# Layer 1's second product as seven block products over three groups of tokens

## The chip, the cores and the metric

The kernel runs on one core of one Trainium2 chip. The metric is device time in microseconds (us) of one execution. Engines are called by their names: TensorE (PE in the rows, its weight load PEld), VectorE (DVE), ScalarE (ACT), GpSimd (POOL), SyncE (SP, whose queue is SPq).

## The reference

Attention with a decay and a causal mask over 4 batches, 8 heads, 576 positions and 64 columns a head; then two layers, each with 2304 tokens, a width of 512 and an inner width of 2048, all in float32:

```python
x = attn(q, k, v, f)                      # 2304 x 512
g = np.maximum(0.01 * (x @ w_in), x @ w_in)
x = g @ w_out                             # layer 1's second product
h = x @ w_in2
x = (h / (1 + np.exp(-h))) @ w_out2       # layer 2
```

The weights come in as 64-bit numbers and are turned into float32 on the chip. A float32 product is made of three matmuls on fp32r parts: each operand is split into a high part (a cast on ScalarE) and a low part (a subtraction, `less`, on VectorE or GpSimd), and high x high, high x low and low x high are summed in PSUM.

## The kernel before

The program holds its own planner, `Plan` (L82). Generators yield operations with an engine, a cost and a rank; the planner runs them in its own time and writes each engine's instructions in the order in which they come out. So the order on every engine, SyncE's transfers included, is fixed ahead. The lowest rank goes first where several operations are ready; `either` (L131) chooses between GpSimd and VectorE by the earlier planned end, with a bonus of 0.3 us for GpSimd. The costs are formulas: `dve_cost` (L244) is 0.07 + 1.042e-3 n us, `pool_cost` 0.1 + 2.2e-3 n. `take` and `give` count buffers; `wait` and `signal` order generators.

The stages overlap. Attention ends near 365 us; layer 1's first product (`hidden`, L929, the hidden product) fills TensorE beside it and runs alone until 404. It goes over eight chunks of tokens; each gated result goes to DRAM as `g1_d`. `conv_out` (L1581), from attention's middle on, turns W_out into float32 in two lines and stores it in `wo_d`; `out_weights` (L1031) loads and splits its 16 row blocks into the weight slots as the last chunk of the hidden product frees them.

The second product, `summed` (L1091), goes over five groups of tokens (256 and 4 x 512). `first_values` (L1054) loads g1 (`gl`) into four buffers and splits it (`gs`) into three. Per group TensorE runs 16 row blocks x 4 column blocks x 3 terms into four PSUM banks; `finish` (L1121) copies the sums out and stores them as `x1_d`.

Layer 2 already uses seven block products. Its first one, `hidden2` (L1338), has 3 groups of 2 x 384 tokens, 8 column pairs and 6 matmuls of 384 columns for each of the seven; its second one, `summed2` (L1477), has matmuls of 256 columns. `fetch2` (L1648) loads its weights' words, `combos` converts and mixes them with four VectorE operations of 256 columns (`sub`, L1174) per pair of row blocks, `second_weights` stores the seven combinations in `w2_d` and `fills` loads and splits them into 28 homes (`unit`, L1619), first for W_in and, as its tiles are used up, for W_out.

Of the kernel before, what the change touches and what calls it, by code (L numbers as in the profile page):

```python
# [53 lines left out]
SUMS = ((0, 256), (256, 512), (768, 512), (1280, 512), (1792, 512))  # L54
SET_A = ("sp", "sp", "sp", "av")
# [205 lines left out]
def fused_kernel(ctx, tc, qt, kt, va, vb, ft, w1, wi2, wo2, out):  # L261
# [9 lines left out]
    NCS = len(SUMS)  # L271
# [21 lines left out]
    wo_d = dram.tile([FF, 128, DM], F32, name="wo_d")  # L293
# [3 lines left out]
    w2_d = dram.tile([2, 128, 2 * NU, 256], F32, name="w2_d")  # L297

    ident = const.tile([128, 128], F32, name="ident")
    zmask = const.tile([128, ZOFF + 256], F32, name="zmask")  # L300
# [241 lines left out]
    at = {}  # L542
# [345 lines left out]
    def attention():  # L888
# [18 lines left out]
        w2t["a"] = ctx.enter_context(tc.tile_pool(name="w2a", bufs=1, side="right"))  # L907
# [100 lines left out]
    def gate(j, s):  # L1008
# [15 lines left out]
        yield dma(1024 * n, lambda: nc.sync.dma_start(out=g1_d[s, :, :, o:o + n], in_=g))  # L1024
# [6 lines left out]
    def out_weights():  # L1031
        def split(f, w, i):
            i_y = yield take("wy", WY_BUFS)
            y = decp["wo"].tile([128, DM], F32, tag="wy", name="wz", bufs=WY_BUFS)
            yield dma(262e3, lambda: nc.sync.dma_start(out=y, in_=wo_d[f]), 0)
            yield copy(DM, w[:, 0], y, "a", 0)
            yield less(DM, w[:, 1], y, f32(w[:, 0]), "pd", 0, PE_LAT)
            give("wy", i_y)
            wo_h[f] = w, i
            signal(("woh", f))  # L1040

        yield wait("weights")
        for f in range(FF):
            i = yield take(("w", ROOM_W[f]), 1)
            w = slot(ROOM_W[f], [128, 2, DM], F32R, "wo")
            p.start(split(f, w, i))
        yield wait(*[("woh", f) for f in range(FF)])
        wo_es.close()
        w2t["b"] = ctx.enter_context(tc.tile_pool(name="w2b", bufs=1))
        signal("decoded")  # L1050

    gs = {}

    def first_values():  # L1054

        yield wait(("ring_free", max(j for j in range(NCH) if j % 2 == 0)))

        def split(j, s, n, cuts, src, i):
            flat = src.rearrange("p a t -> p (a t)")
            for parts in cuts:  # L1060
# [11 lines left out]
        def splits():  # L1072
            yield wait("gated")
            for j, (_, n) in enumerate(SUMS):
                for s in range(NST):
                    yield wait(("gl", j, s))
                    yield from split(j, s, n, ((0, 1),) if n <= T else ((0,), (1,)), *loaded.pop((j, s)))
# [727 lines left out]
```

## Time and profile before

| | us |
|---|---|
| median of 3 runs | 969.61 (967.44 to 971.61) |
| the profiled execution | 969.07 |
| its span, first to last instruction | 967.3 |
| TensorE busy | 955.8 |
| VectorE busy | 669.3 |
| ScalarE busy | 573.7 |
| GpSimd busy | 56.1 |

Busy time counts an instruction from start to end; matmuls overlap in the engine, so the mean duration of one (390 ns for 512 columns) is longer than the time that it adds to a row of them. The pace of a loop is read from busy time by count. Idle time stands in front of the instruction that came late, with the one that released it.

### The profile page before, as it was taken

How to read it: one execution, taken by the hardware profiler on the slowest of the kernel's cores; microseconds unless marked ns; L12 is line 12 of the kernel's file. 1: busy time of each engine (PE TensorE's matmuls, PEld its weight loads, DVE VectorE, ACT ScalarE, POOL GpSimd, SP SyncE). 2: the span in 40 equal slices, each digit the busy share in tenths (PEclk: the TensorE clock that was granted, in tenths of full speed). 3: DMA queues.
4: the chain of work that ended last, by engine and by line, in shares of the span. 5: the costliest groups of instructions: out<-in, count | busy, mean ns of one | idle time of the engine just before them, and what ended most of it. 6: DMA issues, size and time to landing. Idle time of an engine off the chain costs nothing.

```text
span 967.3 us, 18030 instructions
## 1 busy us (share of the span) xinstructions
PE 955.8 (99%) x6433; PEld 878.2 (91%) x6433; DVE 669.3 (69%) x1645; ACT 573.7 (59%) x1296; POOL 56.1 (6%) x73
## 2 busy tenths in 40 slices
PE   9999999999999999999999999999999999999998
PEld 8787998889888989998888888999999999999998
DVE  5998786698669940477787677424144488998884
ACT  7978787788578842644343345546456665454441
POOL 2001220122013000000000000000000020000000
PEclk9999999999999999999999999999999999999999
DMA  7943543476666634789888887552366674554442
GB/s 216 288 130 89 168 155 103 136 229 208 207 188 229 217 117 152 252 305 328 328 306 300 293 319 256 190 192 98 122 205 218 218 221 128 153 154 140 126 128 67
DMA packets 140374, 190.50 MB, mean 197 GB/s; under 512 B 9446, under 2 KB 105342, under 8 KB 140252
## 3 DMA queue, kind: packets, MB, share of 16 engines
q1 hardware_dynamic: 139852, 188.95, 60.3%
q8 instruction: 51, 0.84, 0.4%
q10 hardware_dynamic: 432, 0.39, 0.1%
q14 instruction: 39, 0.32, 0.1%
HBM read 122.79 MB, written 66.50 MB: 196 GB/s over the span
## 4 chain that ended last, share of the span: by engine, by line
PE 77%; DVE 10%; DMA 6%; ACT 5%; issue 2%; SPq 0%; DVEq 0%; ACTq 0%
PE m L1338 18%; PE m L1477 17%; PE acc L1107 17%; PE hpw L929 12%; PE sps L711 4%; PE av L860 4%; PE tps L792 3%; DMA qk<-in_kt_dram 2%; DMA wst<-in_wo_dram 2%; DVE sc L691 2%; ACT sc L734 1%; DMA wst<-in_w_dram 1%; PE hps L929 1%; ACT sc L744 1%; DVE sc L742 1%
## 5 line engine op out<-in xcount | busy, mean ns | idle before, releaser
L929 PE MATMUL hpw<-ring,w 128*128 128x320 f32 (+1 forms) x1344 | 216.0, 303 | 0.1
L1107 PE MATMUL acc<-gs,wo 128*128 128x512 f32 (+1 forms) x960 | 199.0, 369 | 0.7 <-ACT gs L1065 0.4
L1107 PEld LDWEIGHTS acc<-gs,wo 128*128 128x128 f32 x960 | 167.3, 189 | 30.6 <-ACT gs L1065 0.6
L929 PEld LDWEIGHTS hpw<-ring,w 128*128 128x128 f32 x1344 | 189.1, 190 | 2.0 <-issue 1.0
L1338 PE MATMUL m<-xa,w 128*128 128x384 f32 x576 | 113.9, 339 | 1.0 <-ACT m L1364 0.8
L1477 PE MATMUL m<-w,xa 128*128 128x256 f32 x924 | 113.2, 281 | 0.7 <-DVE xa L340 0.6
L1477 PEld LDWEIGHTS m<-w,xa 128*128 128x128 f32 x924 | 110.7, 188 | 1.4 <-DVE xa L340 1.3
L734 ACT ACTIVATE sc<-sc,st 128x576 f32<-128x576 f32 (+4 forms) x160 | 93.1, 582 | 25.2 <-DVE st L691 24.3
L1338 PEld LDWEIGHTS m<-xa,w 128*128 128x128 f32 x576 | 102.0, 188 | 2.3 <-ACT m L1364 1.1
L691 DVE CUSTOM_DVE_ANT_0 sc<-sps,zmask 128x288 f32<-128x288 f32 (+4 forms) x160 | 71.1, 449 | 32.6 <-PE sps L711 23.9
L1065 ACT CAST gs<-gl 128x512 fp32r<-128x512 f32 x72 | 44.6, 621 | 72.2 <-PE acc L1107 66.5
L1338 PE MATMUL m<-xb,w 128*128 128x384 f32 x432 | 86.9, 336 | 0.0
L325 ACT CAST xa<-g 128x512 fp32r<-128x512 f32 x88 | 49.5, 568 | 47.8 <-PE m L1477 22.8
L1338 PEld LDWEIGHTS m<-xb,w 128*128 128x128 f32 x432 | 76.2, 188 | 0.3 <-ACT z L1378 0.2
L1477 PE MATMUL m<-w,xb 128*128 128x256 f32 x588 | 74.1, 283 | 0.3 <-DVE xb L340 0.3
L1477 PEld LDWEIGHTS m<-w,xb 128*128 128x128 f32 x588 | 72.0, 192 | 0.6 <-DVE xb L340 0.5
L792 PE MATMUL tps<-ident,sc 66*107 66x66 f32 (+3 forms) x480 | 67.7, 269 | 1.6 <-ACT sc L744 1.0
L711 PE MATMUL sps<-m,s 66*128 66x288 f32 (+9 forms) x288 | 66.8, 313 | 1.5 <-DVE st L691 0.8
L1174 DVE TENSOR_TENSOR g<-g 128x256 f32<-128x256 f32 x144 | 61.5, 430 | 8.9 <-DMA g<-g_d 8.0
L340 DVE TENSOR_TENSOR gs<-gl,gs 128x512 fp32r<-128x512 f32 x72 | 49.5, 688 | 23.4 <-ACT gs L1065 23.2
L1022 ACT ACTIVATE gw<-hpw 128x320 f32<-128x320 f32 (+1 forms) x112 | 45.1, 410 | 30.9 <-PE hpw L929 27.2
L792 PEld LDWEIGHTS tps<-ident,sc 66*107 66x107 f32 (+3 forms) x480 | 55.5, 152 | 7.8 <-ACT sc L744 1.8
(129 smaller groups left out, 1308.8 us busy)
## 6 DMA issues: line engine op xcount, KB each, us to landing
g_d<-z SPq DMA_DIRECT2D x24, 768.0 KB
g<-g_d SPq DMA_DIRECT2D x36, 512.0 KB
gl<-g_d SPq DMA_DIRECT2D x32, 512.0 KB
w_d<-f SPq DMA_DIRECT2D x16, 896.0 KB
ws<-w_d SPq DMA_DIRECT2D x56, 256.0 KB
g_d<-gw SPq DMA_DIRECT2D x32, 320.0 KB
wst<-in_w_dram SPq DMA_DIRECT2D x17, 512.0 KB
g_d<-gw SPq DMA_DIRECT2D x32, 256.0 KB
```

The costliest lines, as they stand in the source:

```text
L325: ("act", act_cost(n, base), lambda: nc.scalar.copy(dst, src), 0.0),
L340: ("dve", dve_cost(n), lambda: nc.vector.tensor_tensor(dst, a, b, op=ALU.subtract), 0.0),
L691: yield dve(w, lambda: nc.vector.tensor_tensor_reduce(out=sc[0:qn, k0:k0 + w], in0=ps[0:qn], in1=zmask[0:qn, z0:z0 + w], scale=-0.125, sca ...
L711: nc.tensor.matmul(ps[0:qn], ht[x][:, qs], ht[y][:, k0:k0 + w], start=r == 0, stop=r == len(ops) - 1)
L734: yield act(kn, lambda: nc.scalar.activation(sc[0:qn, 0:kn], sc[0:qn, 0:kn], ACTF.Exp, scale=-1.0, bias=st[0:qn, 2 * i + a:2 * i + a + 1], ...
L792: nc.tensor.transpose(ps[0:k1 - k0, o:o + qn], ht["p"][i][0:qn, k0:k1], ident[0:qn, 0:qn])
L929: nc.tensor.matmul(dst, w[:, wi, c * 128:(c + 1) * 128], x(xi, c), start=(first_ and c == 0 and r == 0), stop=(c == KC - 1 and r == 2), sk ...
L1022: yield act(n, lambda: nc.scalar.activation(g[:, part], hp_t, ACTF.Prelu, alpha=0.01), 1, 0.05)
L1107: nc.tensor.matmul(acc[c], w[:, wi, c * 128:(c + 1) * 128], g[:, gi], start=(f == 0 and r == 0), stop=(f == FF - 1 and r == 2), skip_group ...
L1174: ("dve", dve_cost(n), lambda: nc.vector.tensor_tensor(dst, a, b, op=op_), 0.0),
L1338: nc.tensor.matmul(dst, w[:, wi, c * 128:(c + 1) * 128], x[:, xi, c], start=start and c == 0 and r == 0, stop=stop and c == 1 and r == 2, ...
L1477: nc.tensor.matmul(banks[b][:, e], t[:, gi, a * 128:(a + 1) * 128], w[:, wi], start=begin and a == 0 and r == 0, stop=jp == NP // 2 - 1 an ...
```

## The change

Layer 1's second product g @ W_out is cut into 2 x 2 blocks in all three directions: the inner width into 2 x 1024, the output columns into 2 x 256, and the tokens into three groups of 2 x 384. Per group, seven block products stand for eight, on sums and differences of the blocks of g and of W_out.

- W_out: `conv_out` is one line with one buffer. For each of eight pairs of row blocks it converts both, mixes them (`mix`, four VectorE operations of 256 columns) and stores the seven combinations in a third part of `w2_d`. `fills(0)` loads and splits them into the 28 homes that layer 2's weights take later; W_in of layer 2 moves into a home when the last group has used it.
- g: `quarters` loads the blocks a11, a21, a22 and a12 of a group in 4 pieces each (128 x 2 x 384, 48 loads in all) into three sets of homes, which later groups and other blocks take over. `made` and `prep` build the sums in place: x5 = a21 + a22 (VectorE or GpSimd), x6 = x5 - a11, x3 = a12 - x6, x7 = a22 - x6, and split each operand into one of four buffers (`SPLITS`): 84 splits of 768 columns.
- `summed` runs the products in the order of `G_TURN`, 12 matmuls of 384 columns for each piece. `sums` copies partial sums between PSUM banks (seed) and out of them, and adds.
- Layer 2's W_out words are fetched only after product 2 of the last group. Layer 2's tiles move to other homes, its operand combinations are formed in place in another order, and the splits in `fills` may all go to GpSimd.

```diff
-SUMS = ((0, 256), (256, 512), (768, 512), (1280, 512), (1792, 512))
-SET_A = ("sp", "sp", "sp", "av")
+GQ = (1, 5, 6, 2, 7, 4, 3)
+G_TURN = (
+    ((1, 0), (5, 1), (6, 2), (2, 3), (7, 4), (4, 6), (3, 7)),
+    ((1, -2), (6, 1), (5, 2), (2, 3), (7, 4), (4, 6), (3, 7)),
+    ((1, -2), (6, 1), (5, 2), (2, 3), (7, 4), (4, 5), (3, 6)),
+)
+SPLITS = 4
+X_ON = "pd"
...
-    wo_d = dram.tile([FF, 128, DM], F32, name="wo_d")
...
-    w2_d = dram.tile([2, 128, 2 * NU, 256], F32, name="w2_d")
...
+    w2_d = dram.tile([3, 128, 2 * NU, 256], F32, name="w2_d")
...
-        yield dma(1024 * n, lambda: nc.sync.dma_start(out=g1_d[s, :, :, o:o + n], in_=g))
+        yield dma(1024 * n, lambda: nc.sync.dma_start(out=g1_d[s, :, :, o:o + n], in_=g), -1 if j > NCH - 3 else 1)
...
-    def out_weights():
...
-    def first_values():
...
+    def q_group(n, name):
+        return {"11": 0, "21": 1 + n % 2, "12": 1 + n % 2, "22": 2 - n % 2}[name]
+
+    def quarters():
+
+        yield wait("decoded")
+        todo = [(0, "11"), (0, "21"), (0, "22")]
+        for n in range(NG):
+            todo += [(n, "12")]
+            if n + 1 < NG:
+                todo += [(n + 1, "11"), (n + 1, "21"), (n + 1, "22")]
...
+                def load(n, name, s, sg, o, t):
+                    yield dma(393e3, lambda: nc.sync.dma_start(out=t, in_=g1_d[sg, :, :, o:o + TB]), 0)
+                    signal(("q", n, name, s))
+
+                p.start(load(n, name, s, sg, o, quarter(grp, s)))
+
+    g_order = sorted((7 * n + pos, n, q) for n in range(NG) for q, pos in G_TURN[n])
...
+    def q_used(n, name, s, uses):
+
+        k = n, name, s
+        left[k] = left.get(k, uses) - 1
+        if not left[k]:
+            grp = q_group(n, name)
+            give(("q", grp, s), q_count.setdefault((grp, s), 0))
+            q_count[grp, s] += 1
+            if n == NG - 1 and name != "21":
+                signal(("q_gone", grp, s))
+
...
+    def made(n, s):
+
+        a11, a21, a22 = (quarter(q_group(n, k), s) for k in ("11", "21", "22"))
+        yield wait(("q", n, "21", s), ("q", n, "22", s))
+        yield sub(2 * TB, a21, a21, a22, X_ON, 0, ALU.add)
+        signal(("x5", n, s))
+        yield wait(("gx", n, 1, s))
+        yield sub(2 * TB, a11, a21, a11, "d", 0)
+        signal(("x6", n, s))
+        q_used(n, "21", s, 2)
...
+    def prep(n, q, s, i):
+        a = {k: quarter(q_group(n, k), s) for k in ("11", "12", "21", "22")}
+        t = w2t["s", i % SPLITS]
+        src, name = None, None
...
+            src = a["11"]
+        elif q == 4:
+            yield wait(("q", n, "22", s))
+            src = a["22"]
+        elif q == 2:
+            yield wait(("q", n, "12", s))
+            src = a["12"]
+        else:
+            yield wait(("x3", n, s))
+            src = a["12"]
+        yield act(2 * TB, lambda: nc.scalar.copy(t[:, 0], src), 0, 0.09)
+        yield less(2 * TB, t[:, 1], src, f32(t[:, 0]), "d", 0, PE_LAT)
+        gx[n, q, s] = t, i
+        signal(("gx", n, q, s))
+        if q == 5:
+            q_used(n, "21", s, 2)
+        elif q == 7:
+            q_used(n, "22", s, 2)
+            q_used(n, "11", s, 1)
+        elif q == 4:
+            q_used(n, "22", s, 2)
+        elif q == 2:
+            yield wait(("x6", n, s))
+            yield sub(2 * TB, a["12"], a["12"], a["11"], "d", 0)
+            yield wait(("gx", n, 6, s))
+            signal(("x3", n, s))
+        elif q == 3:
+            q_used(n, "12", s, 1)
+
+    def preps():
+        yield wait("decoded")
+        for n in range(NG):
+            for s in range(SF):
+                p.start(made(n, s))
+        for _, n, q in g_order:
+            for s in range(SF):
+                i = yield take("split", SPLITS)
+                p.start(prep(n, q, s, i))
+
+    G_BANKS = (("sp", "sp"), ("sp", "av"), ("h", "h"), (("acc", 0), ("acc", 1)))
+
+    def g_bank(n, role, j):
+        return bank(G_BANKS[(3 * n + (0, 2, 1)[role]) % 4][j], [128, TB], "acc")
...
-            yield wait("hidden" if j else "attention")
...
-                    yield op("pe", mm_cost(n, 3), lambda: product(c), 1, 0)
...
+            if q == 5:
+                yield wait("hidden", ("second", n, 0), ("second", n, 1))
+                for j in range(2):
+                    held[n][j][1] = yield from g_bank(n, 1, j)
+                signal(("third", n))
+            need = {1: None, 2: "seed1", 6: "seed1", 7: "two1", 4: "three1", 5: None, 3: "four1"}[q]
+            role, start, stop = {
+                1: (0, True, False), 2: (0, False, True), 6: (2, False, False), 7: (2, False, False),
+                4: (2, False, True), 5: (1, True, False), 3: (1, False, True),
+            }[q]
+            for s in range(SF):
+                k = SF * GQ.index(q) + s
+                yield wait(("gx", n, q, s), ("wu", k))
+                x, i = gx[n, q, s]
+                w = wu[k]
...
+                    def product():
+                        for e in range(2):
+                            for r, (wi, xi) in enumerate(((0, 0), (0, 1), (1, 0))):
+                                nc.tensor.matmul(
+                                    dst, w[:, e, wi, j * 128:(j + 1) * 128], x[:, xi, e],
+                                    start=start and s == 0 and e == 0 and r == 0,
+                                    stop=stop and s == SF - 1 and e == 1 and r == 2, skip_group_check=True,
+                                )
+
+                    yield op("pe", 6 * MMB, product, 1 if "hidden" in p.seen else 2, 0)
+                    if s == SF - 1:
+                        signal(("m1", n, j, q))
+                give("split", i)
...
+    def sums(n, j, held):
+        c_t, c_h = held[0]
+        held[2] = yield from g_bank(n, 2, j)
+        signal(("second", n, j))
...
+        yield wait(("m1", n, j, 1))
+        yield act(TB, lambda: nc.scalar.copy(y_t, c_t), -1, 0.1)
+        signal(("seed1", n, j))
...
+        yield wait(("m1", n, j, 5))
+        v_t, v_h = held[1]
+        yield dve(TB, lambda: nc.vector.tensor_tensor(z, v_t, z, op=ALU.add), -1)
+        signal(("four1", n, j))
+
...
+
+        p.start(fourth())
+        yield wait(("m1", n, j, 4))
+        p.start(evict(y_t, 1, j, y_h))
+        yield wait(("m1", n, j, 3))
+        yield dve(TB, lambda: nc.vector.tensor_tensor(u, v_t, u, op=ALU.add), 0)
+        give(*v_h)
...
+    def mix(f, b12, rank):
+        yield sub(HW, f[:, 4], f[:, b12], f[:, 0], "d", rank)
+        yield sub(HW, f[:, b12], f[:, 3], f[:, b12], "d", rank)
+        yield sub(HW, f[:, 5], f[:, 3], f[:, 4], "d", rank)
+        yield sub(HW, f[:, 6], f[:, 3 - b12], f[:, 5], "d", rank)
+
...
+    def conv_out():
+        out_d = w2_d[0].rearrange("p (s f) n -> p s f n", s=7)
+        for j in range(FF // 2):
+            yield wait(("words1", j, 0))
+            i_f = yield take("wf", 1)
+            f = decp["wo"].tile([128, 7, HW], F32, tag="wf", name="wf", bufs=1)
+            y = f[:, 4:6].rearrange("p s n -> p (s n)")
+            for e in range(2):
+                yield wait(("words1", j, e))
+                src, i_s = words1.pop((j, e))
+                t = f[:, 2 * e:2 * e + 2].rearrange("p s n -> p (s n)")
+                yield from to_f32(t, src, y, t, 2, True)
+                give("wst", i_s)
+            yield from mix(f, 1, 2)
+            yield dma(918e3, lambda: nc.sync.dma_start(out=out_d[:, :, j], in_=f), 2)
+            give("wf", i_f)
+            signal(("spilt", 0, j))
...
-    UNIT_AT = ["ring1"] * 4 + [("w", r) for r in ROOM_W] + ["g"] * 3 + ["ring0"] * 4 + [("u", 0)]
+    UNIT_AT = ["ring0"] * 4 + [("w", r) for r in ROOM_W] + [("u", 0)] + ["ring1"] * 4 + ["g"] * 3
...
+            if which:
+                yield wait(("m1", NG - 1, 1, 2))
...
+    def fills(which):
+        for u in range(NU):
+            if which == 0:
+                q, s = GQ[u // SF], u % SF
+                at_ = 8 * W_SLOT[1][q] + 2 * s
+                yield wait(*[("spilt", 0, 2 * s + e) for e in range(2)])
+            else:
+                at_ = 2 * u
+                both = (2 * u, 2 * u + 1)
+                yield wait(*[("spilt", which, n // 7) for n in both])
+                yield wait(*([("used", n // 7, W_Q[0][n % 7]) for n in both] if which > 1 else [("used1", u)]))
+                units[which - 1, u][1]()
+            t = yield from unit(which, u)
+
+            def fill(u, at_, t):
+                rank = 1 if which else 0
+                src = f32(t[:, :, 1])
+                yield dma(262e3, lambda: nc.sync.dma_start(out=src, in_=w2_d[which, :, at_:at_ + 2]), rank)
+                yield act(2 * HW, lambda: nc.scalar.copy(t[:, :, 0], src), rank)
+                yield less(2 * HW, t[:, :, 1], src, f32(t[:, :, 0]), "pd", rank, PE_LAT)
+                if which == 0:
+                    wu[u] = t
+                    signal(("wu", u))
+                    return
...
```

## Rows read from the trace of the kernel before

**Rows 1.** The page's part 1: busy us (share of span) x instructions, by engine.
```profile
PE 955.8 (99%) x6433; PEld 878.2 (91%) x6433; DVE 669.3 (69%) x1645; ACT 573.7 (59%) x1296; POOL 56.1 (6%) x73
```
**Rows 2.** TensorE groups by shape: busy us, mean ns of one, idle us before, its releasers.
```profile
L1107 PE MATMUL acc<-gs,wo 128*128 128x512 f32 x768 | 175.4, 390 | 0.0
...
L1338 PE MATMUL m<-xa,w 128*128 128x384 f32 x576 | 113.9, 339 | 1.0 <-ACT m L1364 0.8 <-DVE ev L1130 0.2
...
L1338 PE MATMUL m<-xb,w 128*128 128x384 f32 x432 | 86.9, 336 | 0.0
...
L1107 PE MATMUL acc<-gs,wo 128*128 128x256 f32 x192 | 23.8, 285 | 0.7 <-ACT gs L1065 0.4 <-DVE gs L340 0.3
```
**Rows 3.** The chain that ended last, in order of time: start us, us, what.
```profile
398.62 3.18 DMA wz<-wo_d
...
531.52 8.44 DMA wst<-in_wo_dram
...
613.32 164.78 PE m L1338 x936
```
**Rows 4.** VectorE groups by shape in 404 to 610, columns as in rows 2.
```profile
L340 DVE TENSOR_TENSOR gs<-gl,gs 128x512 fp32r<-128x512 f32 x72 | 49.5, 688 | 23.4 <-ACT gs L1065 23.2
L1174 DVE TENSOR_TENSOR f<-f 128x256 f32<-128x256 f32 x64 | 26.0, 421 | 0.8
L1524 DVE SCALAR_TENSOR_TENSOR f<-f 128x512 int32<-128x512 int32 x32 | 22.1, 691 | 0.9
L1526 DVE SCALAR_TENSOR_TENSOR f<-wst,f 128x512 int32<-128x512 int32 x32 | 22.1, 689 | 0.7
L1523 DVE TENSOR_SCALAR f<-f 128x512 int32<-128x512 int32 x32 | 13.6, 424 | 18.0 <-ACT f L1522 17.9
...
L340 DVE TENSOR_TENSOR xb<-x1s,xb 128x768 fp32r<-128x768 f32 x1 | 1.0, 955 | 0.0
...
L1382 DVE TENSOR_TENSOR z<-m,z 128x384 f32<-128x384 f32 x1 | 0.6, 550 | 0.0
```
**Rows 5.** Stretches: PE, PEld, DVE, ACT, POOL busy (x), clock, DMA share, GB/s.
```profile
200.00:350.00 150.00, 147.38 (x1103) 133.61 (x1103) 118.53 (x370) 113.37 (x304) 23.50 (x26) 1.00 0.65 209
...
365.00:609.00 244.00, 243.10 (x1278) 212.13 (x1278) 162.56 (x289) 105.81 (x186) 0.00 (x0) 1.00 0.82 283
613.00:777.00 164.00, 163.68 (x931) 163.53 (x932) 65.30 (x99) 94.99 (x179) 0.00 (x0) 1.00 0.55 180
800.00:960.00 160.00, 160.00 (x1353) 159.91 (x1352) 134.92 (x289) 74.83 (x137) 0.00 (x0) 1.00 0.44 129
```
**Rows 6.** Timeline, VectorE and GpSimd, 780 to 793: start us, us, engine, line, operation.
```profile
781.98 1.62 POOL L336 TENSOR_TENSOR w<-ws,w 128x256 fp32r<-128x256 f32 x2 [471.36 <-ACT w L1708]
782.19 0.81 DVE L1174 TENSOR_TENSOR g<-g 128x256 f32<-128x256 f32 x1
782.92 1.23 DVE L340 TENSOR_TENSOR xa<-g,xa 128x512 fp32r<-128x512 f32 x1
...
784.07 0.41 DVE L1174 TENSOR_TENSOR g<-g 128x256 f32<-128x256 f32 x1
...
784.41 0.68 DVE L340 TENSOR_TENSOR xa<-g,xa 128x512 fp32r<-128x512 f32 x1
```
**Rows 7.** ScalarE groups by shape in 404 to 610, columns as in rows 2.
```profile
L1065 ACT CAST gs<-gl 128x512 fp32r<-128x512 f32 x71 | 44.0, 621 | 72.2 <-PE acc L1107 66.5 <-issue 3.3 <-DVE f L1174 2.1
...
L1203 ACT CAST xa<-xs 128x768 fp32r<-128x768 f32 x2 | 1.7, 830 | 1.6 <-DVE xs L1174 1.6
```
**Rows 8.** Waits of SyncE's queue in 404 to 612: us in total, times, longest us.
```profile
SPq L1686 <- DVE f L1174: 40.1, 14, 7.6
```
**Rows 9.** Timeline, 340 to 412: last W_out store issued, attention's last write.
```profile
346.67 0.32 SPq L1593 DMA_DIRECT2D wo_d<-wy  x1
...
364.82 0.49 DVE L340 TENSOR_TENSOR ring<-av,ring 128x320 fp32r<-128x320 f32 x1 [3.40 <-ACT ring L325]
```

More of the change, by code (lines that the diff above doesn't have):

```diff
@@ L1177, in second_input @@
     def second_input():
-        yield wait("attention")
+        yield wait("decoded")
         for g in range(NG):
-            yield wait(*[("x1", j) for j, (o, n) in enumerate(SUMS) if o < 2 * TB * (g + 1) and o + n > 2 * TB * g])
+            yield wait("decoded", *[("x1", g, i, c) for i in range(2) for c in range(KC)])
             if g:
@@ L1216, in second_input @@
             a22 = st[1]
-            i_xs = yield take("xs", 1)
-            xs = w2t["a"].tile([128, 2, TB], F32, tag="xs", name="xs")
-            yield sub(2 * TB, xs, a21, a22, "d", 1, ALU.add)
-            p.start(split(5, xs))
-            yield sub(2 * TB, a21, a11, a21, "d", 1)
-            p.start(split(7, a21))
-            p.start(split(4, a22, st_i[1]))
+            yield sub(2 * TB, a21, a21, a22, "d", 1, ALU.add)
+            p.start(split(5, a21))
             yield wait(("x1s", g, 1, 0))
@@ L1227, in second_input @@
             yield wait(("xc", g, 5))
-            yield sub(2 * TB, xs, xs, a11, "d", 0)
-            p.start(split(6, xs))
+            yield sub(2 * TB, a21, a21, a11, "d", 0)
+            p.start(split(6, a21))
+            yield wait(("xc", g, 1))
+            yield sub(2 * TB, a11, a22, a21, "d", 0)
+            p.start(split(7, a11))
+            p.start(split(4, a22, st_i[1]))
             yield wait(("xc", g, 2))
-            yield sub(2 * TB, a12, a12, xs, "d", 0)
+            yield sub(2 * TB, a12, a12, a21, "d", 0)
             p.start(split(3, a12, st_i[0]))
             yield wait(*[("xc", g, q) for q in QO])
-            give("xs", i_xs)
             give("f", i_f)
@@ L1313, in hidden2 @@
     def hidden2():
-        yield wait("attention")
+        yield wait("decoded")
         held = {}
@@ L1318, in hidden2 @@
                 if n < 2:
-                    yield wait(("set", NCS - 2 + n))
+                    yield wait(*[("second", NG - 1, k) for k in range(2)], *([("third", NG - 1)] if n else []))
                 held[n] = [(yield from bank2(n, 0)), None, None]
@@ L1371, in gate2 @@
         signal(("two", n))
[L1372 to L1374 removed]
+        yield wait(("m", n, 2))
+        z, i_z = yield from z_room()
         yield silu(z[:, 2], c_t, TB)
@@ L1721, in second_weights, with all_fills @@
             yield par(*[line(which, todo) for _ in range(F_BUFS)])
-            if not which:
-                yield wait("decoded")
-                p.start(fills(1))
         signal("wo2_made")
+    def all_fills():
+        yield wait("decoded")
+        for which in range(3):
+            yield from fills(which)
     wo_es = ctx.enter_context(ExitStack())
@@ L1749, in fused_kernel @@
     with tc.manual_schedule():
-        for gen in (opening(), first_weights(), loads(), attention(), hidden(), out_weights(), first_values(), summed(),
+        for gen in (opening(), first_weights(), loads(), attention(), hidden(), quarters(), preps(), summed(), all_fills(),
                     second_input(), second_weights(), hidden2(), second_values(), summed2()):
```

386 lines of the change are left out of this document (194 added, 192 removed).

## The prediction

> **What bounds the kernel now.** I read the page's busy shares first: TensorE is busy 99% of the span, VectorE 69%, ScalarE 59% [rows 1]. So the time is TensorE's queue, and a change pays by what it takes out of that queue, less the new places where the queue stands still. Then the TensorE groups by shape, to price the removed loop and a loop of the new shape [rows 2], and the chain that ended last, which holds a long unbroken piece of the new shape and two loads [rows 3]. Then VectorE, the next engine: its groups in the stretch of the product [rows 4], its share by stretch, with the granted clock at 1.00 in each [rows 5], and its price where GpSimd runs beside it [rows 6]. Last ScalarE's casts [rows 7], SyncE's queue, which issues nearly every transfer in order [rows 8], and the end of attention [rows 9].
>
> **TensorE, removed.** The loop at L1107 has 768 matmuls of 512 columns and 192 of 256: 175.4 + 23.8 = 199.2 us, with 0.7 us of idle at its start, where a split was late: 199.9 us [rows 2].
>
> **TensorE, added.** 3 groups x 7 products x 4 row pairs x 2 column halves x 2 x 3 terms = 1008 matmuls of 384 columns. That is the count (576 + 432) and the shape of layer 2's first product at L1338 [rows 2], so that loop is the price. Its long piece in the chain takes 164.78 us for 936, 0.1760 us each [rows 3]: 177.5 us, with two seed matmuls 177.9 us. A wider stream is a little cheaper per column: 512 columns take 175.4 / 768 = 0.228 us [rows 2], 0.446 ns a column against 0.458; that is why 7/8 of the columns gives 0.89 of the time. **Net: -22.0 us** if TensorE never waits. The product starts at 404.2 as now and would end at 582 instead of 604 in TensorE time of its own.
>
> **VectorE from the end of attention to the end of the product.** This term decides. Before it is 162.6 of 244 us (365 to 609), two thirds [rows 5]. The edits, with a 512-column two-input operation at 0.688 us, 256 at 0.421, 768 at 0.955, 384 from PSUM at 0.55 [rows 4]:
> - out: the 72 gs splits (49.5), ten eviction copies (6), 16 W_out splits (11.0), and the conversion of layer 2's W_out, half of 26.0 + 22.1 + 22.1 + 13.6, so 41.9, which now waits for a product of the last group: 108.4;
> - in: 84 splits of 768 (80.2), three combinations in place for each of 12 row pairs (36 x 0.955, 34.4), 12 additions out of PSUM (6.6), 28 W_out splits (19.3), and 12 sums a21 + a22 (11.5), which may go to GpSimd: 152.0.
>
> So 162.6 - 108.4 + 152.0 = 206 us, in a stretch that shrinks from 244 to 217 us (365 to 582): 95%. ScalarE takes 84 casts at 0.83 us (70) for 72 at 0.62 (44) [rows 7] and 30 PSUM copies for ten; at 105.8 of 244 us before [rows 5] it has room, cost 0.
>
> What of the 206 us can slip past 582? Layer 2's W_in is needed one column pair per 7.4 us (42 matmuls at 0.176), so the later half of its 28 splits (9.6 us) and the conversion of the last two pairs (2 x 5.2) may come after: 20 us. Then it is 186 of 217, 86%. The trace shows that VectorE at 84% over 160 us (134.9, in 800 to 960) costs TensorE nothing [rows 5]. But there ten pair buffers lie between the two; the new loop has four split buffers of 2.1 us of TensorE each, 8.4 us of lead. And the order on each engine is written out ahead with costs too small for VectorE: dve_cost (L244) gives 0.870 us for 768 columns and 0.603 for 512, where the trace has 0.955 and 0.688, so VectorE falls a tenth behind wherever that order fills it. Bounds: 0 (all covered) to 20 us (nothing slips); I take **+6**, nearer to the row of 84% than to the full count.
>
> **GpSimd's part.** Sums and weight splits may run there ("pd"). Beside a GpSimd split, VectorE's 512-column subtraction took 1.23 us, and 0.68 in the next turn without one; the 256-column one 0.81 against 0.41 [rows 6]. GpSimd's own 512 columns took 1.62 us and cost VectorE 0.40 + 0.55 = 0.95 us, more than the 0.69 that they cost on VectorE itself. So 20 of the 56 weight splits there add 20 x 0.26 = 5 us to VectorE, which lies inside the bounds above. The Trainium skill has a rule that speaks against this edit, on its page "Perfetto Trace Analysis", section "Optimizing Scalar/DVE Operations": GpSimd and VectorE share an SBUF read port, so offloading between the two might not help. By that rule nothing is won there, and the trace agrees (1.23 against 0.68 us); were it wrong, 12 sums and 20 splits would leave VectorE at 161 of 217 us, 74%, and the sum would be 952.
>
> **Homes that come free late.** A group's a22 quarter goes where the previous group's a12 was, free only after the third product's split. Chain: split (0.83 + 0.955), load, sum 0.955, combination 0.955, split 1.8. A load under this traffic took 3.18 us (256 KB) to 8.44 us (512 KB) [rows 3], and SyncE's queue stood up to 7.6 us behind a spill that waited for VectorE [rows 8]. So 8 to 13 us on free engines, against seven turns of TensorE, 14.8 us, between the home's release and the use. Two such changes of group: each 0 to 6 us, I take 1.5: **+3**. Of SyncE's issues, 48 quarter loads stand for 40 loads and 28 weight loads for 16; behind a held one queue the spills and layer 2's words, for which nobody on TensorE waits before 582.
>
> **Attention's stretch.** Mixing W_out adds 32 operations of 256 columns, 13.5 us, to VectorE, which had 118.5 of 150 us in 200 to 350 [rows 5]: 79% to 88%. TensorE's cover there is the hidden product; it was idle 2.6 us in those 150 [rows 5]. The conversion becomes one line with one mixing buffer; its last store was issued at 346.7, attention's last write is at 364.8 [rows 9], and if it now ends later, the first group's loads start then. Until 395 or so the hidden product covers that. Bounds 0 to 8 (half of the added work exposed); **+1.5**. The start itself: 0.7 us was lost there before [rows 2]; **+0.5**, bounds 0 to 3.
>
> **After the product** nothing changes in count. Layer 2's W_out conversion (41.9 us of VectorE, 16 loads and 8 spills) lands in 613 to 777, where VectorE has 65.3 of 164 us and DMA a share of 0.55 [rows 5]: cost 0; were it late, the last product would wait, 0 to 5.
>
> **Sum.** The profiled execution took 969.07 us, 967.3 of span and 1.8 around it, 0.5 below the median of 969.61. 969.07 - 22.0 + 6 + 3 + 1.5 + 0.5 = 958.1.
>
> **Rivals.**
> 1. *Full cover.* VectorE's work slips past the product, and four buffers of lead are enough, as at 84% now [rows 5]. Waits 1 to 4 us: 948 to 951; **950**. Against it: 95% before slipping, and costs planned a tenth low.
> 2. *VectorE half binds.* The order doesn't let the W_in conversion slip (12), and the group changes cost 4 us each (8): 969 - 22 + 20 = **967**, no change. For it: conversion is put into every gap that the planned order shows.
> 3. *VectorE becomes the bound, slower.* Place: 365 to the end of the product. Before 404 transfers limit it: 16 quarters, 20 weight loads and the last hidden columns are some 16 MB, and 39 us at the stretch's 283 GB/s [rows 5] bring 11, so some 12 of the 39 us stay idle. Then 365 + 206 + 12 + 12 (GpSimd, 48 operations at 0.26) = 595, with the group changes at 6 each and attention's 3 it is 610, against 604 now: **975**. It decides from the point where VectorE's work that can't slip, with its gaps, passes 239 us (604 - 365). Against it: 20 us can slip.
> 4. *The change doesn't save what it says:* the 384-column stream is slower here than at L1338; at 0.198 us each the cut is gone. No row speaks for it; it is held within rival 2.
>
> **How the numbers follow.** Forecast (952 to 964.8) 0.48; full cover 0.17; half bound 0.20, of which 0.02 falls below 964.8; slower 0.15. Range 947 to 974: it takes in rivals 1 and 2 and leaves out most of rival 3. A measurement of this kernel tells about 0.5%, 4.8 us, from no change. Faster by more 0.67, within 0.18, slower 0.15.
>
> **What would show it.** The product's group has 1008 matmuls and pieces at 0.176 us; its idle by releaser splits the stalls: VectorE's split says rivals 2 or 3, a quarter's load says the homes. VectorE's share from 365 to the end of the product is near 90%, and near 88% in 200 to 350 with TensorE idle under 5 us. I am wrong if TensorE idles over 20 us in the product, if the granted clock falls there, or if the last product waits for layer 2's W_out.

## The result and the profile after

The changed kernel takes 976.91 us in the median of 6 runs (974.26 to 979.21), the kernel before 969.37 in 6 runs beside it: 1.0075 times the time, 95% interval 1.0052 to 1.0097. That is slower by 7.5 us, where 958.1 was forecast and the range ended at 974: the time is that of rival 3 (975). The profiled execution took 974.26 us.

Part 1 of the page after, busy us (share of the span) and instructions, answers [rows 1]:

```profile
PE 943.0 (97%) x6483; PEld 891.2 (92%) x6483; DVE 765.3 (79%) x1752; ACT 609.6 (63%) x1382; POOL 127.1 (13%) x126
```

TensorE is busy 12.8 us less than before and yet ends later: its idle time rose from 11.5 to 29.6 us. VectorE rose by 96 us, GpSimd by 71. The TensorE groups after (busy us, mean ns, idle us in front, releasers), to be held against [rows 2]:

```profile
L1193 PE MATMUL acc<-gs,w 128*128 128x384 f32 x1008 | 187.0, 344 | 13.2 <-DVE gs L348 6.4 <-DVE w L348 3.5 <-ACT ev L1264 1.4
L1491 PE MATMUL m<-xc,w 128*128 128x384 f32 x1008 | 181.4, 340 | 3.8 <-ACT ev L1234 2.0 <-DVE xc L348 1.8
```

The product is there as described, 1008 matmuls, but 187.0 + 13.2 = 200.2 us is what the removed loop cost (199.9). The whole cut went into waits, most of them for VectorE's splits, and into matmuls that are busy longer: 187.0 us for a count that was priced at 177.5. The windows of the stretch (busy us of PE, PEld, DVE, ACT, POOL; granted clock; DMA share; GB/s) show where; the last line is the whole stretch:

```profile
390.00:410.00 20.00, 16.11 (x89) 15.54 (x89) 17.13 (x21) 13.05 (x25) 6.53 (x5) 0.91 0.88 288
...
430.00:450.00 20.00, 19.15 (x106) 18.25 (x104) 19.75 (x18) 13.53 (x23) 14.63 (x12) 1.00 0.57 204
...
510.00:530.00 20.00, 20.00 (x115) 20.00 (x115) 19.20 (x29) 11.06 (x17) 0.00 (x0) 1.00 0.70 227
530.00:550.00 20.00, 20.00 (x115) 20.00 (x114) 14.85 (x16) 10.22 (x16) 3.64 (x3) 1.00 0.83 263
...
570.00:590.00 20.00, 15.49 (x77) 14.53 (x76) 20.00 (x17) 13.01 (x21) 16.78 (x14) 0.91 0.47 141
590.00:612.00 22.00, 18.58 (x104) 17.92 (x103) 21.07 (x21) 14.79 (x24) 13.35 (x11) 1.00 0.39 114
365.00:612.00 247.00, 229.97 (x1330) 224.39 (x1329) 208.14 (x250) 134.70 (x219) 66.49 (x49) 0.98 0.70 231
```

The largest losses of TensorE, 3.9, 4.5 and 3.4 us, lie where GpSimd (the fifth pair) works, and it runs through where that hardly works (510 to 550). The windows alone don't settle it: from 430 to 450 GpSimd is busy 14.6 us and TensorE loses 0.9, and the windows from 450 to 510, not shown, lose 4.4 us with little of it. From 570 to 590 VectorE is busy all the time and does 17 operations; from 510 to 530 it did 29. Some of those were smaller, so the fair measure is one shape: a 768-column split takes 1.39 us in the mean from 570 to 590, and 0.955 from 510 to 530. VectorE's share from 365 to 612 is 208 of 247 us, only 84%, so the mean alone would not have named it. Its groups in that stretch, beside [rows 4]:

```profile
L348 DVE TENSOR_TENSOR gs<-gq,gs 128x768 fp32r<-128x768 f32 x84 | 89.8, 1079 | 21.2 <-ACT gs L1126 20.6
L1328 DVE TENSOR_TENSOR gq<-gq 128x768 f32<-128x768 f32 x43 | 49.4, 1173 | 4.9 <-DMA gq<-g_d 4.6
L348 DVE TENSOR_TENSOR w<-w 128x512 fp32r<-128x512 f32 x30 | 23.5, 800 | 4.4 <-ACT w L1883 4.1
```

A 768-column split was priced at 0.955 us and takes 1.08 in the mean, a combination (with the sums that stayed on VectorE) 1.17. The timeline of VectorE from 569 on gives the two prices side by side (start us, us, operation):

```profile
569.21 1.49 DVE L348 TENSOR_TENSOR gs<-gq,gs 128x768 fp32r<-128x768 f32 x1
570.62 2.90 DVE L1328 TENSOR_TENSOR gq<-gq 128x768 f32<-128x768 f32 x2
573.44 0.68 DVE L348 TENSOR_TENSOR w<-w 128x512 fp32r<-128x512 f32 x1
...
576.87 1.22 DVE L348 TENSOR_TENSOR w<-w 128x512 fp32r<-128x512 f32 x1
...
582.23 0.95 DVE L348 TENSOR_TENSOR gs<-gq,gs 128x768 fp32r<-128x768 f32 x1
```

and GpSimd's beside it:

```profile
567.19 5.51 POOL L344 TENSOR_TENSOR w<-w 128x256 fp32r<-128x256 f32 x4 [18.27 <-ACT w L1883]
573.64 7.84 POOL L344 TENSOR_TENSOR w<-w 128x256 fp32r<-128x256 f32 x6 [0.94 <-ACT w L1883]
583.76 7.40 POOL L344 TENSOR_TENSOR w<-w 128x256 fp32r<-128x256 f32 x6 [2.27 <-ACT w L1883]
```

A 512-column split that starts in GpSimd's first pause (572.7 to 573.6) takes 0.68 us, and a 768-column one inside the second (581.5 to 583.8) 0.95; beside its pieces they take 1.22 and 1.49. This is [rows 6] again, now on the operations that TensorE waits for. No wait of TensorE, VectorE, ScalarE or SyncE's queue between 365 and 640 ends with GpSimd, so it isn't GpSimd's own results that are late.

### The profile page after: what moved, and what is told of

It reads as the page before. It is cut to its first block, busy times and chain, and to the rows that moved or that the text cites. A ratio compares the mean times of both kernels' runs of the same rounds, so it can differ in the third digit from the quotient of the medians.

```text
span 972.6 us, 18370 instructions
## 1 busy us (share of the span) xinstructions
PE 943.0 (97%) x6483; PEld 891.2 (92%) x6483; DVE 765.3 (79%) x1752; ACT 609.6 (63%) x1382; POOL 127.1 (13%) x126
## 4 chain that ended last, share of the span: by engine, by line
PE 71%; DVE 13%; DMA 7%; ACT 4%; issue 3%; SPq 1%; POOL 0%; DVEq 0%; ACTq 0%; POOLq 0%
PE m L1491 18%; PE m L1634 18%; PE hpw L935 12%; PE acc L1193 11%; PE sps L718 4%; PE av L867 4%; PE tps L799 3%; DVE gs L348 2%; DMA gq<-g_d 2%; DVE gq L1328 2%; DVE sc L698 1%; ACT sc L741 1%; PE hps L935 1%; DMA wsr<-in_w_dram 1%; ACT sc L751 1%
## 5 line engine op out<-in xcount | busy, mean ns | idle before, releaser
L1193 PE MATMUL acc<-gs,w 128*128 128x384 f32 x1008 | 187.0, 344 | 13.2 <-DVE gs L348 6.4
L1193 PEld LDWEIGHTS acc<-gs,w 128*128 128x128 f32 x1008 | 180.7, 191 | 16.9 <-DVE gs L348 8.1
L1491 PE MATMUL m<-xc,w 128*128 128x384 f32 x1008 | 181.4, 340 | 3.8 <-ACT ev L1234 2.0
L1491 PEld LDWEIGHTS m<-xc,w 128*128 128x128 f32 x1008 | 178.1, 188 | 5.4 <-ACT ev L1234 2.3
L1634 PE MATMUL m<-w,gc 128*128 128x256 f32 x1512 | 178.6, 280 | 0.0
L1634 PEld LDWEIGHTS m<-w,gc 128*128 128x128 f32 x1512 | 178.4, 188 | 0.0
L333 ACT CAST gc<-g 128x512 fp32r<-128x512 f32 (+1 forms) x180 | 80.6, 490 | 86.1 <-DVE g L1328 54.9
L1126 ACT CAST gs<-gq 128x768 fp32r<-128x768 f32 x84 | 69.4, 836 | 72.1 <-DVE gq L1328 35.8
L741 ACT ACTIVATE sc<-sc,st 128x576 f32<-128x576 f32 (+4 forms) x160 | 92.9, 581 | 24.8 <-DVE st L698 23.9
L348 DVE TENSOR_TENSOR gs<-gq,gs 128x768 fp32r<-128x768 f32 x84 | 89.8, 1079 | 21.2 <-ACT gs L1126 20.6
L348 DVE TENSOR_TENSOR gc<-g,gc 128x512 fp32r<-128x512 f32 (+1 forms) x180 | 91.3, 532 | 3.2 <-ACT gc L333 2.1
```

The lines of the kernel that those rows point to most:

```text
L333: ("act", act_cost(n, base), lambda: nc.scalar.copy(dst, src), 0.0),
L348: ("dve", dve_cost(n), lambda: nc.vector.tensor_tensor(dst, a, b, op=ALU.subtract), 0.0),
L741: yield act(kn, lambda: nc.scalar.activation(sc[0:qn, 0:kn], sc[0:qn, 0:kn], ACTF.Exp, scale=-1.0, bias=st[0:qn, 2 * i + a:2 * i + a + 1], ...
L1193: nc.tensor.matmul(dst, w[:, e, wi, j * 128:(j + 1) * 128], x[:, xi, e], start=start and s == 0 and e == 0 and r == 0, stop=stop and s == ...
L1491: nc.tensor.matmul(dst, w[:, wi, c * 128:(c + 1) * 128], x[:, xi, c], start=start and c == 0 and r == 0, stop=stop and c == 1 and r == 2, ...
L1634: nc.tensor.matmul(banks[b][:, e], t[:, gi, a * 128:(a + 1) * 128], w[:, wi], start=begin and a == 0 and r == 0, stop=jp == NP // 2 - 1 an ...
```

## The experiments

Five theories. **A**: VectorE bounds the product because GpSimd, to which the change lets weight splits and sums go, slows it. **B**: it is bound by the sheer new work. **C**: the order is made with costs too small, so that it can't be kept. **D**: pieces of the product queued between hidden matmuls wait for late weights. **E**: quarter loads and homes are late. Times are medians; ratios are to the kernel before, run beside each.

| kernel | us | ratio, 95% interval |
|---|---|---|
| after | 976.9 | 1.005 to 1.010 |
| no_gpsimd | 957.1 | 0.985 to 0.990 |
| sums_on_vector | 971.2 | 0.999 to 1.003 |
| splits_on_vector | 963.1 | 0.988 to 0.995 |
| gpsimd_one_column | 952.1 | 0.980 to 0.986 |
| before_gpsimd | 970.2 | 0.998 to 1.002 |
| no_combos | 957.2 | 0.985 to 0.991 |
| no_filler | 969.4 | 0.999 to 1.001 |
| no_gpsimd_no_filler | 960.0 | 0.987 to 0.992 |
| true_costs | 986.3 | 1.013 to 1.021 |
| no_gpsimd_true_costs | 975.0 | 1.003 to 1.008 |
| no_gpsimd_order | 964.3 | 0.993 to 0.997 |
| no_gpsimd_costs_order | 976.2 | 1.005 to 1.010 |

**no_gpsimd.** Two places, both in the change: the sums' engines and the weight splits'.

```diff
-X_ON = "pd"
+X_ON = "d"
-    yield less(..., f32(t[:, :, 0]), "pd", rank, PE_LAT)
+    yield less(..., f32(t[:, :, 0]), "d" if which < 2 else "pd", rank, PE_LAT)
```

> Edit: the sums a21 + a22 and the 56 weight splits between 365 and 620 us run on VectorE alone; GpSimd does nothing there. The changed kernel takes 976.9 us, the kernel before 969.4. Theory A (VectorE is the bound of the product because GpSimd slows it): VectorE's excess beside GpSimd is about 25 us by the trace after (768 columns at 1.36 to 1.50 us beside GpSimd against 0.95 without), and the work that comes to it instead is about 22 us (25 splits at 0.69, 5 sums at 0.955), so VectorE's busy time in 365 to 612 stays near 208 us within 6, and the time comes out between 965 and 977, below the middle if the two dense GpSimd stretches (430 to 450, 570 to 612) were where the product stood still. Theory B (VectorE is bound by the sheer new work): 974 to 980. If the offload to GpSimd was a real gain, VectorE becomes busier by 20 us and the time rises to 985 or more.

It takes 957.1 us: 19.8 below after and 12.2 below the kernel before. That is more than A had asked for, and B, which asked for 974 to 980, is out. Part 1 of its page:

```profile
PE 940.5 (98%) x6483; PEld 889.9 (93%) x6483; DVE 755.8 (79%) x1779; ACT 610.4 (64%) x1382; POOL 61.1 (6%) x77
```

Its TensorE groups:

```profile
L1193 PE MATMUL acc<-gs,w 128*128 128x384 f32 x1008 | 185.2, 342 | 6.6 <-DVE gs L348 4.4 <-ACT gs L1126 0.9 <-DVE w L348 0.8
L1491 PE MATMUL m<-xc,w 128*128 128x384 f32 x1008 | 180.3, 339 | 0.0
```

Its windows where after stood (columns as above):

```profile
570.00:590.00 20.00, 19.97 (x113) 19.33 (x112) 19.69 (x26) 18.89 (x32) 0.00 (x0) 1.00 0.53 158
590.00:612.00 22.00, 22.00 (x126) 21.86 (x125) 17.32 (x31) 9.01 (x17) 0.00 (x0) 1.00 0.40 119
```

From 570 to 590 VectorE does 26 operations instead of 17 in the same time, its 768-column splits at 0.954 us each, and TensorE hardly waits there. This version beats both kernels.

**sums_on_vector, splits_on_vector.** One of the two places each.

```diff
-X_ON = "pd"
+X_ON = "d"
```

> Edit: of the two loosened rules of the change only one goes back: the sums a21 + a22 run on VectorE alone; the weight splits may still go to GpSimd. After: 976.9 us; with neither on GpSimd 957.1. In the trace after, the 5 sums on GpSimd were 11.8 us of its work in the stretch and the 25 splits 60.0. If the cost goes with GpSimd's busy time, the sums bear 16% of the 20 us: 972 to 976. Rival (a few long sums at the head of a group are what stops TensorE, the splits being small pieces): 960 to 966.

```diff
-    yield less(..., f32(t[:, :, 0]), "pd", rank, PE_LAT)
+    yield less(..., f32(t[:, :, 0]), "d" if which < 2 else "pd", rank, PE_LAT)
```

> Edit: the other half: the 56 weight splits up to the second layer's first set run on VectorE alone, the sums may still go to GpSimd. If the cost goes with GpSimd's busy time, 84% of the 20 us comes back: 957 to 962. Rival (the sums are what stops TensorE): 970 to 976.

5.7 us and 13.8 us below after; together 19.5 of the 19.8. Neither half alone is the cause. Both times lie just outside what a price by GpSimd's busy time asked for: the five sums bear 29% of the cost with 16% of that time. The traces show most of the difference: held against the same instructions in gpsimd_one_column (next), the VectorE operations beside the five sums are 7.1 us longer, 1.4 a sum, and those beside the 25 splits 23.5, 0.94 a split, so the sums have 23% of the slowing. The last 1 us may be the order, which is another one in each of these kernels.

**gpsimd_one_column.** The order of every engine is that of after, instruction by instruction, and all waits are; only GpSimd's pieces after attention are shorter. Left out: all but one column of each of those splits and sums (of each half in a sum). The edit of the splits is shown; that of the sums is alike.

```diff
-    nc.gpsimd.tensor_tensor(dst[:, s_], a[:, s_], b[:, s_], op=ALU.subtract)
+    nc.gpsimd.tensor_tensor(dst[:, s_, 0:1], a[:, s_, 0:1], b[:, s_, 0:1], op=ALU.subtract)
```

> The changed kernel with every engine's instructions in the same order and with the same waits; only GpSimd's pieces after attention (weight splits and sums) are cut to one column of each row, so the low parts and sums that it should make are not made and the numbers differ. It separates the two halves of the price: here VectorE gets none of GpSimd's work and is not slowed by it. Theory A (sharing is what costs): VectorE's 768-column splits come back from 1.08 us in the mean to 0.96, its busy time in 365 to 612 falls by some 20 us, and the time comes to 952 to 958, at or below no_gpsimd's 957.1, where VectorE does the 22 us itself. Rival (the order that the loosened rule makes is bad in itself, GpSimd's length is not the matter): 968 or more.

952.1 us, as A said. Since no other instruction is touched, VectorE's busy time tells what the sharing took. Part 1 of its page:

```profile
PE 935.0 (99%) x6483; PEld 887.6 (94%) x6483; DVE 736.6 (78%) x1752; ACT 609.4 (64%) x1382; POOL 84.3 (9%) x126
```

TensorE's group of the product:

```profile
L1196 PE MATMUL acc<-gs,w 128*128 128x384 f32 x1008 | 181.9, 339 | 2.9 <-DVE gs L351 1.2 <-ACT gs L1129 1.1 <-DVE w L351 0.6
```

The same 1752 VectorE instructions take 736.6 us here and 765.3 in after: 28.7 us of sharing, and 24.8 us of time. From here to no_gpsimd VectorE takes on 19.2 us of GpSimd's work at full speed (755.8 us in 1779 instructions), and the time rises by only 5.0. So a microsecond of slowing cost 0.86 us (24.8 / 28.7), and a microsecond of added work 0.26. The first is a little high: 2.3 of the 24.4 us between the two profiled executions were lost in the first 100 us, where the kernels are alike, which leaves 0.77. The second is less certain, since no_gpsimd has an order of its own. The likely reason, argued from the windows and not tried by itself: an added split is put where its own due time allows, but the planner sends work to GpSimd when VectorE's queue is long, so what is slowed is the piece that TensorE is about to need.

**before_gpsimd.** The same sharing where VectorE has room.

```diff
-    yield less(..., "pd" if which and u >= 20 else "d", rank, PE_LAT)
+    yield less(..., ("pd" if u >= 20 else "d") if which else "p", rank, PE_LAT)
```

> The kernel before, with the 28 splits of layer 2's first weights moved from VectorE to GpSimd (19.3 us of VectorE work leave). VectorE is busy 154 of 206 us in its product there (404 to 610). Theory A says that sharing lengthens VectorE's operations whatever its load (28 splits of two pieces, some 1 us of excess each: VectorE 154 - 19 + 28 = 163 us), and that this costs time only where VectorE has no slack: with 163 of 206 us busy TensorE hardly waits, 968 to 974. Rival (GpSimd's pieces hold up TensorE's stream directly, or are late themselves): 980 or more.

970.2 us, no change. Part 1 of its page:

```profile
PE 956.6 (99%) x6433; PEld 878.2 (91%) x6433; DVE 658.9 (68%) x1617; ACT 574.7 (59%) x1296; POOL 102.0 (11%) x129
```

GpSimd's group of these splits, from 380 to 650:

```profile
L336 POOL TENSOR_TENSOR w<-ws,w 128x256 fp32r<-128x256 f32 x56 | 46.1, 853 | 279.8 <-PE acc L1107 133.5 <-DVE z L1382 124.9 <-ACT w L1708 21.4
```

VectorE gave up 28 splits, 19.3 us, and its busy time fell by 10.4 from [rows 1]: 8.9 us of sharing, which TensorE doesn't feel. That is 0.32 us a split, a third of what was expected (VectorE is busy 149.0 us from 404 to 610, not 163): only 45% of GpSimd's time there lies beside a VectorE operation, against 96% in after. At 0.86 us each the 8.9 us would have cost 7.7. So neither GpSimd nor the sharing is the cost as such, but the sharing in a stretch in which VectorE's queue is behind.

**no_combos.** Left out: the 36 combinations in place, their lines deleted and their waits kept.

```diff
-    yield sub(2 * TB, a11, a21, a11, "d", 0)
-    yield sub(2 * TB, a["11"], a["22"], a["11"], "d", 0)
-    yield sub(2 * TB, a["12"], a["12"], a["11"], "d", 0)
```

> Left out: the 36 combinations in place (a21 - a11, a11 - a22, a12 - x), so the products take uncombined quarters and the numbers differ; every load, split, matmul and wait stays. Theory A and B (VectorE is the bound of the product): 36 operations of 0.95 to 1.4 us, some 34 to 45 us, leave VectorE, and the 20 us that 960 matmuls of the product took beyond 169 us come back for the most part: 955 to 962. Theory E (late quarter loads, homes that come free late): less than 4 us, 973 to 977, since the loads keep their times.

957.2 us. VectorE lost 33.9 us of busy time and the time 19.7: VectorE it is, and not the loads as such (E), though a shorter queue on VectorE also frees the homes sooner. The planner then sent only 16 splits and no sum to GpSimd (39.6 us in 365 to 612 instead of 66.5), so this run can't part A from B; gpsimd_one_column does.

**no_filler, no_gpsimd_no_filler.**

```diff
     yield wait(("gx", n, q, s), ("wu", k))
+    if n == 0 and q == 1 and s == 0:
+        yield wait("hidden")
```

> Edit: no matmul of the product but the two seeds is queued on TensorE before the hidden product has ended. Theory D (the pieces that the order puts between hidden matmuls wait for weights that come late): the idle 0.4 + 3.5 us at 392 to 396 goes and the time falls by 3 to 6 us, to 971 to 974. Rival: the hidden product only ends earlier and the same weights and splits are late after it; then VectorE's queue decides and the time is unchanged, 975 to 979, or longer by what the pieces filled.

7.5 us below after, more than the 3.9 of that wait, so D seemed to hold. VectorE's timeline ahead of it in after:

```profile
386.06 8.74 DVE L1328 TENSOR_TENSOR gq<-gq 128x768 f32<-128x768 f32 x6 [4.64 <-DMA gq<-g_d]
...
395.79 0.68 DVE L348 TENSOR_TENSOR w<-w 128x512 fp32r<-128x512 f32 x1
```

GpSimd's timeline beside it:

```profile
387.58 4.67 POOL L1327 TENSOR_TENSOR gq<-gq 128x768 f32<-128x768 f32 x2 [52.91 <-DMA gq<-g_d]
```

The two of these six that run beside GpSimd's sums take 2.41 and 2.60 us instead of 0.96, and the split that TensorE waits for (3.49 us, at 396.5) is queued behind them. In no_gpsimd seven of the same operations take 6.17 us, and the split starts at 391.16:

```profile
385.07 6.17 DVE L1328 TENSOR_TENSOR gq<-gq 128x768 f32<-128x768 f32 x7
391.16 0.68 DVE L348 TENSOR_TENSOR w<-w 128x512 fp32r<-128x512 f32 x1
```

So the early pieces should cost nothing once GpSimd is out, which the second run tried (the last group's partial sums are in the u buffers there):

> no_gpsimd, with no matmul of the product but the two seeds queued before the hidden product has ended, as in no_filler (and the last group's partial sums in the same buffers as the other groups', so that an order can be made). no_filler took 7.5 us off after, of which 3.9 were idle at 392 to 396. In no_gpsimd TensorE waits only 1.5 us there, so at most 1 to 2 us are to be had: 955 to 958. Rival (the pieces queued early cost by themselves, whatever GpSimd does): 948 to 952.

960.0 against 957.1, with intervals that overlap: no gain, and outside both of the ranges given. So D is most likely a consequence of A; the other u buffers came with this run, and layer 2's first product waits 2.3 us for a ScalarE copy (`u`, L1524) that had waited for the store out of such a buffer, which it doesn't in no_gpsimd.

**true_costs** and three kernels after it.

```diff
+    def dve_cost(n, fast=False):
+        return (0.155 if "attention" in p.seen else 0.07) + n * (0.52e-3 if fast else 1.042e-3)
```

> Edit: from the end of attention on, the order is made with a VectorE cost of 0.155 us plus 1.042 ns a column (0.955 us for 768 columns, as measured without GpSimd) instead of 0.07; so that the order can be made at all, layer 2's first input is fetched after the last store of its converted weights, and the last weights' words after the first input. Theory C (costs planned too low make an order that VectorE can't keep): the product's idle shrinks and the time falls to 966 to 972. Theories A and B (VectorE has too much to do whatever the order): 973 to 980.

9.3 us above after, the wrong way for C. GpSimd is busy 94.1 us from 365 to 640 there, against 66.5 in after (the next expectation gives that stretch as 365 to 612): a dearer VectorE sends it more.

> Edit: no_gpsimd, and from the end of attention on the order is made with the VectorE costs that true_costs had (0.955 us for 768 columns). true_costs alone was 9 us slower than after; its order gave GpSimd 94 us of work in 365 to 612 instead of 66, because a dearer VectorE sends more there. If that was all that was wrong with it, the truer costs without GpSimd leave at most the stalls that no_gpsimd still has (6.6 us in the product) to gain: 950 to 957. Rival (the cost has nothing to do with the stalls, or it places other work badly): 957 to 964.

975.0, a miss too: without GpSimd the costs still lost 18 us. But the edit that lets the order be made came with them, so the last pair parted the two (the first input waits here for the last words of the first weights, in the two runs above for their last store):

```diff
     if g:
         yield wait(("m", NP * g - STAGE_LEAD[g - 1], 7))
+    else:
+        yield wait(("words2", 0, NP - 1, 1))
-    yield wait(("m1", NG - 1, 1, 2))
+    yield wait(("m1", NG - 1, 1, 2), "last_u", ("x1s", 0, 1, 0))
```

> Control for the next kernel: no_gpsimd, with layer 2's first input fetched only after the last words of its first weights, and the last weights' words after that input. It moves a few loads at 560 to 620 us. Expected within 3 us of 957.1; if it rises by 8 us or more with a wait of layer 2's first product for its split input, then what made no_gpsimd_true_costs slow (8.1 us at 590 to 612) was this and not the costs.

> no_gpsimd_order with the truer VectorE costs from the end of attention on. Theory C (part of the 6.6 us that TensorE still waits in the product comes from costs planned a tenth low): 2 to 6 us below no_gpsimd_order. Rival: no difference within 2 us, or longer, since what is planned later also starts later.

964.3 and 976.2. Moving a few loads costs 7.2 us (the first bound of that expectation was missed), the costs another 11.9. TensorE's group of the product in the first:

```profile
L1193 PE MATMUL acc<-gs,w 128*128 128x384 f32 x1008 | 184.9, 341 | 10.2 <-DVE gs L348 4.8 <-ACT gs L1126 4.3 <-DVE w L348 0.8
```

Both of its groups in the second:

```profile
L1496 PE MATMUL m<-xc,w 128*128 128x384 f32 x1008 | 185.0, 344 | 11.1 <-ACT xc L1362 9.6 <-DVE xc L351 1.1 <-ACT u L1527 0.4
L1196 PE MATMUL acc<-gs,w 128*128 128x384 f32 x1008 | 182.5, 341 | 4.9 <-DVE gs L351 2.9 <-ACT gs L1129 1.7 <-ACT ev L1267 0.4
```

The truer costs did what C says inside the product (195.1 to 187.4 us), and more than gave it back: at the second layer's first product TensorE now waits 11.1 us, 9.6 of them for the cast of its input, which had itself waited for its load. Probably the conversion of layer 2's weights, last in rank, comes later with VectorE dearer, and the input's loads behind it; that was not tried. So C holds in the product, and as tried it gains nothing in the whole. That a few moved loads cost 7.2 us also says how much of a difference between two orders may be the order; only gpsimd_one_column keeps it.

## Why the prediction was wrong

**The step that failed is "GpSimd's part".** It priced a split on GpSimd at 0.95 us of VectorE time, took off the 0.69 that it would cost there, and put 20 x 0.26 = 5 us "inside the bounds above", so nothing of it entered the sum. The 0.95 was right for a split beside a busy VectorE (0.94 above, 0.32 where VectorE was often idle). In VectorE's busy time the subtraction holds too: 765.3 against 755.8 us, 9.5 for the 27 operations that no_gpsimd moved, 0.35 each. What failed is to take it for the time: 28.7 us of slowing cost 24.8 us, and the same work on VectorE 5.0, so running it on GpSimd cost 19.8, where nothing was put. The sum as it stands is that of a kernel without this step, and no_gpsimd ran it: 958.1 forecast, 957.1 measured. How good that is, the other steps show.

The Trainium skill's page "Perfetto Trace Analysis", section "Optimizing Scalar/DVE Operations", says that moving work between the two "might not help". The trace bears it out, and more than that: it cost 19.8 us. I had quoted it and used it only to argue that nothing is won.

**The other steps**, read in no_gpsimd, where that one is absent:

- *TensorE, -22.0.* The removed loop was right. The added one was a little too cheap: with no wait at all the 1008 matmuls at L1491 are busy 180.3 us, and layer 2's loop before, counted in the same way over both of its groups, 179.0, not the 177.5 of one long piece of [rows 3]. So the cut is nearer to 20.6.
- *VectorE, +6; homes, +3; the start, +0.5.* These 9.5 us came out as 6.8, every wait of TensorE between 365 and 612. The start has 0.29 + 0.45 + 0.77 = 1.5, inside its bound; after had 3.9 at the last two, by GpSimd. The other five waits:

```profile
444.36 35.67 PE L1193 MATMUL acc<-gs,w 128*128 128x384 f32 x192 [1.76 <-DVE gs L348]
480.83 4.41 PE L1193 MATMUL acc<-gs,w 128*128 128x384 f32 x23 [0.81 <-DVE gs L348]
486.10 0.44 PE L1193 MATMUL acc<-gs,w 128*128 128x384 f32 x1 [0.85 <-ACT gs L1126]
487.84 62.65 PE L1193 MATMUL acc<-gs,w 128*128 128x384 f32 x348 [1.30 <-DVE gs L348]
551.04 22.35 PE L1193 MATMUL acc<-gs,w 128*128 128x384 f32 x125 [0.55 <-DVE gs L348]
```

  The whole stretch (columns as above):

```profile
365.00:612.00 247.00, 240.15 (x1401) 235.52 (x1398) 204.91 (x291) 139.13 (x228) 0.00 (x0) 0.99 0.73 239
```

  The three waits between 480 and 488, 3.0 us, follow two loads of a group change in the chain, which begin when a split has freed the home:

```profile
463.05 6.71 DMA gq<-g_d
469.76 0.94 DVE gs L348
470.70 0.02 issue
470.72 4.65 DMA gq<-g_d
```

  So the homes have their +3, if all of it is theirs (VectorE works without a pause from 475 to 488, too), and VectorE alone has the 1.76 and 0.55, 2.3 and not 6. Its share was near what was reckoned after slipping, 83% (204.9 of 247) for 86%, but TensorE waits in bursts. Probably that is because four split buffers carry little from one burst to the next: VectorE's splits idle 16.3 us there, nearly all of it behind casts, and the casts' longest wait is for TensorE to free a buffer. The sign that I named, a share near 90%, failed in after too (84%).
- *Attention, +1.5.* TensorE is busy 262.3 us of 100 to 365 before and 260.9 in no_gpsimd: 1.4. VectorE has 84% of 200 to 350 (125.6 of 150 us), not 88%, and TensorE is idle 3.4 us there against 2.6 before.
- *The sum of these:* 969.1 - 20.6 + 6.8 + 1.4 = 956.7. The hit of 958.1 is in part luck, as the cut was 1.4 us too large and the waits 2.7. The execution read here took 960.03 us, 3.3 more than this sum: 1.8 of them go with the granted clock of 0.91 in its window from 430 to 450, the rest was not found.
- *Not in the sum:* what a stall does to the clock. A falling clock was named as a sign of being wrong, and came, but had no price. In after the granted clock was 0.91 in 570 to 590, after three waits of TensorE, so part of that window ran at 1.2 GHz and not 2.4; the 1008 matmuls are busy 187.0 us, against 181.9 in gpsimd_one_column, where the clock stayed at 1.00. So 5.1 us, most of them by the clock, came on top of the 10.3 us by which the product's idle differs (13.2 against 2.9). The second layer's group differs by 1.4 us of busy time and 3.8 of idle.

**Rival 3** had the time, the place and the engine. Its reckoning filled the stretch with VectorE's work and took 12 us for GpSimd; the trace has 28.7 us of sharing, bursts, and a VectorE that is idle 39 of 247 us. So that 975 came so near to 976.9 is luck in part. It was given 0.15 because 20 us of VectorE's work could slip and GpSimd's price had been netted against VectorE's relief.

**Left open:** after's profiled execution had lost 2.3 us more in the first 100 us (TensorE busy 95.2) than no_gpsimd and gpsimd_one_column (97.5), which run the same opening; no experiment looked at that. Why the moved loads of no_gpsimd_order cost 7.2 us was not tried either.

## What to carry to other kernels

Price work moved from VectorE to GpSimd gross: what it adds to VectorE's operations beside it, not that less the relief, and see whether those are the ones that TensorE waits for; a planner that picks GpSimd when VectorE's queue is long can put the slowing exactly there. A share of 84% over a stretch doesn't show that an engine has room: look at short windows (20 us did here, where the buffers between the two engines hold 8.4 us by the prediction's estimate), and hold the mean duration of one shape in them against that in a quiet window, as well as the busy time. To price sharing cleanly, keep every instruction in its order and shrink only the suspected engine's pieces.

## What was not expected of the hardware

Sharing slows both engines at once: a 768-column two-input VectorE operation goes from 0.95 to 1.49 us beside GpSimd's weight splits (2.41 and 2.60 beside its 768-column sums), and GpSimd's 256-column piece takes 1.23 us in the mean of after (50 pieces, 60.0 us) where it took 0.85 in before_gpsimd beside a less busy VectorE. A GpSimd piece of one column still takes 0.53 us (50 pieces, 25.5 us, in gpsimd_one_column). And stalls of 1 to 2 us can cost TensorE more than their length, by the clock that is granted behind them: 0.83 in 580 to 590 of after, with three waits of 1.1, 1.6 and 1.8 us since 577, and 0.91 in 430 to 450 of no_gpsimd, with one of 1.76 at 444. Not each does: the wait of 1.8 us at 451 in after left it at 1.00.
